# An attention and gated-MLP kernel: query blocks aligned to key tiles, and longer DMA transposes

## The chip, the cores and the metric

The kernel runs on one core of a Trainium2 chip. The metric is the device time of one execution in microseconds (us). A core has a matrix engine (TensorE, PE in the profile, with its weight loads shown as PEld), a vector engine (DVE), a scalar engine (ACT), GpSimd (POOL) and SyncE (SP), which here only issues transfers. Each engine works through its own queue in order and waits on semaphores. 16 DMA engines move data; transfers issued by SP, ACT and POOL share them. A profiled execution on the chip gives the rows quoted below.

## The reference

Eight batches with eight heads, 576 tokens each, head size 64. The keys and values are 16 beacon tokens, which every query sees, followed by the batch's own 576, which are causal. The attention output, with heads side by side, is the input of a gated MLP over all 4608 tokens.

```python
k_all = concat([beacon_k, k], axis=2)            # 16 + 576 keys
v_all = concat([beacon_v, v], axis=2)
scores = (q @ k_all.T) / sqrt(64)                # causal over the 576, beacons always seen
a = softmax(where(causal, -1e9, scores))
x = (a @ v_all)                                  # -> [4608, 512], 8 heads x 64 wide
out = (gelu(x @ w_gate) * (x @ w_val)) @ w_out   # 512 -> 1536 -> 512, output float32
```

Inputs are float32; inside, the kernel works in bfloat16 with float32 accumulation.

## The kernel before

**Attention.** Heads go in pairs, so that one pair's two heads of 64 stand in the two halves of the 128 partitions. A batch has four pairs (`m`). Queries and keys must stand with the head dimension on the partitions; that is `qkT`, one buffer for the batch at work. Scores are computed with keys on the partitions: for each of five key tiles (128, 128, 128, 128 and 80 rows, the first 16 of tile 0 being the beacons) against the queries that may see it. Because of the 16 beacons, the query blocks that start at a key tile's diagonal begin at 0, 112, 240, 368 and 496 (`S_LO`). A pair's scores come in four chunks (`CHUNKS`), each with one exponential on ACT; GpSimd then zeroes the masked triangle of each diagonal block (in batch 0 a matmul with `neg` does it). `attend` multiplies the exponentials with the values, with a column of ones that gives the denominator; DVE divides (`normalize`) and leaves `y_sb`, with query rows on the partitions and two heads side by side.

**Turning the result.** The MLP needs `xT_sb`, the model dimension on the partitions. In batches 1 to 7 the first three pairs are turned by DMA transposes on SP's queue (`turn_dma`, L368, two for each pair: 112 queries, then four blocks of 128). The fourth is turned by PE (`turn`, L180) and copied by DVE (`put`, L386). In batch 0 all four go through PE.

**Turning queries and keys.** Batches 0 and 1 are turned by PE (`tr_part`, tile `t_ps`). From batch 2 on, `transpose_dma` (L238) issues ten DMA transposes on SP's queue, five blocks of queries and five of keys, from buffers that GpSimd's transfers (L108, cast to bfloat16) filled one batch earlier.

**The MLP.** Nine chunks of 512 tokens (`ci`). `gate_val` makes one of 12 tiles of the hidden dimension: four matmuls for the gate, four for the value, GELU on ACT, product on DVE. `out_mms` makes the output; the matmuls of chunk b-1 are dealt out in portions, `o(n)`, between the attention steps of batch b, 48 in all for each batch.

**Order.** Every instruction's place is written out by hand and kept (`keep`). The loop over `b` has, in this order: ACT's table load, score chunks with portions of `out_mms`, `av_head` and `av` for the pairs, `turn_dma` for each, the fourth pair, the table load for GELU, then the first two gate tiles with the contraction steps `kk` in the order 0, 3, 1, 2, so that the pair whose DMA is last comes last. Then come the other ten tiles. After the first two tiles GpSimd's `hold` (L378) reads the columns of pair 2 in `xT_sb`: as POOL's queue is in order, the loads behind it (values of b+1, queries and keys of b+2) start only when that transpose has landed. The transposes of batch b+1 are issued in the same place. Stores of the output tiles go out where `store` stands, twice per batch on ACT's queue and twice on SP's. A DMA waits for the one eight places earlier on its kind of queue.

**The start.** The float32 queries and keys of batch 0's first pair come by SP's and ACT's queues into `raw` and are cast by ACT and DVE; all others come by GpSimd's transfers, already cast. 56 matmuls on zeros (`warm`) run on PE meanwhile, and eight filler transposes between the first key and query transposes.

Of the kernel before, what the change touches and what calls it, by code (L numbers as in the profile page):

```python
# [7 lines left out]
P = 128  # L8
B, H, S, NB, D = 8, 8, 576, 16, 64
SK = S + NB  # L10
# [11 lines left out]
S_LO = [0, 112, 240, 368, 496]  # L22
KROWS = [128, 128, 128, 128, 80]
DIAG = [112, 128, 128, 128, 80]
# [4 lines left out]
    [(0, 512, 64, 0), (2, 240, 336, 64), (4, 496, 80, 400)],  # L29
    [(1, 112, 464, 0)],  # L30
    [(3, 368, 208, 0)],
]
CHUNK_W = [512, 480, 464, 208]
CHUNK_OFF = [0, 512, 992, 1456]
EXP_W = 1664

EXP_OFF = [0, 992, 576, 1456, 912]
DV = D + 1

Q_N = [128, 128, 128, 128, 80]  # L40
# [11 lines left out]
def kernel(  # L52
# [17 lines left out]
    npool = ctx.enter_context(tc.tile_pool(name="npool", bufs=4))  # L70
    fpool = ctx.enter_context(tc.tile_pool(name="fpool", bufs=3))
# [14 lines left out]
    xT_sb = const.tile([P, NPAIR, N_TOK + P - Q_N[4]], BF16, name="xT_sb", tag="xT_sb")  # L86

    exp_ring = ring.tile([P, NPAIR, 2, EXP_W + P - Q_N[4]], BF16, name="expT", tag="expT")
# [13 lines left out]
    qkT = ring.tile([P, NPAIR, 2, 640], BF16, name="qkT", tag="qkT")  # L102
    nc.vector.memset(qkT[:, :, 1, SK:640], 0.0)

# [7 lines left out]
    def qk6_of(b):  # L112
        if b not in qk6:
            qk6[b] = (
                hpool.tile([P, 2, H, 6 * D], BF16, name="qk6", tag="hT_sb"),
                npool.tile([NB, H, D], BF16, name="kb", tag="kb"),
            )
        return qk6[b]
# [12 lines left out]
    def key_loads(src, beacon, dst, b):  # L131
        parts = [
            (dst[0:NB, 0, :, :], beacon[b].rearrange("h t d -> t h d")),
            (dst[NB:P, 0, :, :], src[b, :, 0:112, :].rearrange("h p d -> p h d")),
        ]
        for j in range(1, 5):
            n = KROWS[j]
            r0 = 112 + (j - 1) * P
            parts.append((dst[0:n, j, :, :], src[b, :, r0 : r0 + n, :].rearrange("h p d -> p h d")))
        return [lambda o=o, i=i: dma(o, i) for o, i in parts]  # L140

    def qk_loads(b):
        q_sb, k_sb = q_ring[b % NRING], k_ring[b % NRING]
        parts = []
        for j in range(5):
            n = P if j < 4 else 64
            parts.append(
                (q_sb[0:n, j, :, :], q[b, :, j * P : j * P + n, :].rearrange("h p d -> p h d"))
            )
        return [lambda o=o, i=i: dma(o, i) for o, i in parts] + key_loads(k, beacon_k, k_sb, b)  # L150
# [82 lines left out]
    def transpose_dma(b):  # L233
        q_sb, k_sb = q_ring[b % NRING], k_ring[b % NRING]
        for j in range(5):
            for w, src, n, c in ((0, q_sb, P if j < 4 else 64, NB), (1, k_sb, P if j < 4 else 80, 0)):
                keep(
                    nc.sync.dma_start_transpose(  # L238
                        out=qkT[:, :, w, c + j * P : c + j * P + n],
                        in_=src[0:n, j, :, :].rearrange("p h d -> p (h d)"),  # L240
                    )
                )

# [18 lines left out]
    def score_mms(b, m, c, s_ps):  # L262
        for t, s_lo, w, col in CHUNKS[c]:
            diag = b == 0 and s_lo == S_LO[t]
            for hi in range(2):
                r = slice(64 * hi, 64 * hi + 64)
                mm(
                    s_ps[:, hi, col : col + w],
                    qkT[r, m, 1, t * P : (t + 1) * P],
                    qkT[r, m, 0, NB + s_lo : NB + s_lo + w],  # L270
                    True,
                    not diag,
                    skip_group_check=True,
                )
            if diag:
                base, n = (NB if t == 0 else 0), DIAG[t]
                for k0, width in ((0, min(n, 64 - base)), (64, n)):
                    for hi in range(2):
                        r = slice(64 * hi, 64 * hi + 64)
                        c0 = 64 + 64 * hi - k0  # L280
                        mm(
                            s_ps[:, hi, col : col + width],
                            eye[r, c0 : c0 + P],
                            neg[r, c0 + base : c0 + base + width],
                            False,
                            k0 == 64,
                            skip_group_check=True,
                        )

    def masks(b, m, c):  # L290
        expT = exp_ring[:, m, :, :]
        for t, s_lo, _, _ in CHUNKS[c]:
            if s_lo != S_LO[t]:
                continue
            n = DIAG[t]
            d = expT[0 : KROWS[t], :, EXP_OFF[t] : EXP_OFF[t] + n]
            keep(
                nc.gpsimd.affine_select(  # L298
                    out=d,
                    in_=d,  # L300
                    pattern=[[0, 2], [1, n]],
                    compare_op=ALU.is_ge,
                    fill=0.0,
                    base=NB if t == 0 else 0,
                    channel_multiplier=-1,
                )
            )

    x_of = {}

    def attend(b, m, hi, x_ps):
        expT, v_sb = exp_ring[:, m, :, :], v_ring[b % NRING]
        for j in range(5):
            for t in range(j + 1):
                e0 = EXP_OFF[t] + S_LO[j] - S_LO[t]
                mm(
                    x_ps[:, j * DV : (j + 1) * DV],
                    expT[0 : KROWS[t], hi, e0 : e0 + P],
                    v_sb[0 : KROWS[t], t, 2 * m + hi, 0:DV],
                    t == 0,  # L320
                    t == j,
                    skip_group_check=True,
                )
# [3 lines left out]
    def normalize(b, m, x_ps, h0, h1):  # L327
        i = b * NPAIR + m
        if h0 == 0:
            y_of[i] = npool.tile([P, 5, 2, D], BF16, name="y_sb", tag="y_sb")  # L330
# [23 lines left out]

    def turn(b, m, pool=None, tag="t"):
        y_sb = y_of[b * NPAIR + m].rearrange("p j e d -> p j (e d)")
        y_ps = (pool or psum_t).tile([P, 1024], BF16, name="y_ps", tag=tag)
        y_of[b * NPAIR + m] = y_ps
        for j in range(5):
            n = Q_N[j] if j else S_LO[1]  # L360
            tr(y_ps[:, S_LO[j] : S_LO[j] + n], y_sb[0:n, j, :])

    def turn_dma(b, m):
        y_sb = y_of.pop(b * NPAIR + m)
        n0 = b * S
        for n, j0, j1, q0 in ((S_LO[1], 0, 1, 0), (P, 1, 5, S_LO[1])):
            keep(
                nc.sync.dma_start_transpose(  # L368
                    out=xT_sb[:, m, n0 + q0 : n0 + q0 + n * (j1 - j0)].rearrange("p (j n) -> p j n", n=n),
                    in_=y_sb[0:n, j0:j1, :, :].rearrange("p j e d -> p (j e d)"),  # L370
                )
            )

# [6 lines left out]
    def put(b, m, by_act=False):  # L380
        y_ps = y_of.pop(b * NPAIR + m)
        out_ap = xT_sb[:, m, b * S : (b + 1) * S]
        if by_act:
            act(out_ap, y_ps[:, 0:S], ACT.Copy)
        else:
            keep(nc.vector.tensor_copy(out_ap, y_ps[:, 0:S]))  # L386
# [87 lines left out]
    raw = [opool.tile([P, 4, D_MODEL], FP32, name="raw", tag="o_sb") for _ in range(2)]  # L474
    raw0 = [raw[w][0:96, 0:2, 0 : 6 * D] for w in range(2)]
    for w, engine in ((1, nc.sync), (0, nc.scalar)):
        keep(
            engine.dma_start(
                out=raw0[w], in_=(q, k)[w][0, 0:2, :, :].rearrange("h (p r) d -> p h (r d)", r=6)
            )  # L480
        )
    kb_sb, vb_sb = (raw[1][0:NB, g, :].rearrange("t (h d) -> t h d", h=H) for g in (2, 3))
    keep(nc.sync.dma_start(out=kb_sb, in_=beacon_k[0].rearrange("h t d -> t h d")))
    keep(nc.sync.dma_start(out=vb_sb, in_=beacon_v[0].rearrange("h t d -> t h d")))
    load_qk6(0, 2, 4, (1,))
# [39 lines left out]
    warm(56)  # L525
    act(qk6[0][0][0:96, 1, 0:2, :], raw0[1], ACT.Copy)
    keep(nc.vector.tensor_tensor_scan(neg, eye, idle, -1.0, ALU.add, ALU.add))
    keep(nc.vector.tensor_scalar_mul(neg, neg, -MASKED))
    keep(nc.vector.tensor_copy(qk6[0][1], kb_sb))
    keep(nc.vector.tensor_copy(qk6[0][0][0:96, 0, 0:2, :], raw0[0]))  # L530
    transpose_both(0, 0)
    keep(nc.vector.tensor_copy(v_ring[0][0:NB, 0, :, 0:D], vb_sb))
# [36 lines left out]
    for b in range(B):  # L569
# [6 lines left out]
        if b:  # L576
# [13 lines left out]
            store(nc.scalar)  # L590
# [14 lines left out]
            store(nc.scalar)  # L605
# [10 lines left out]
            o(7)  # L616
            store(nc.sync)
            turn(b, 3)
            put(b, 3)
            o(4)  # L620
            keep(nc.scalar.preload_act_table_set(SET_GELU))
            for kk in (0, 3, 1, 2):
                for fi in range(2):
                    gv_mms(b, fi, kk, last=kk == 2)
        for fi in range(F_TILES):
# [4 lines left out]
            if fi == 0:  # L630
                store(nc.sync)
                if b and b + 1 < B:
                    hold(b, 2)
# [3 lines left out]
                if 2 <= b + 1 < B:  # L637
                    transpose_dma(b + 1)
    for fi in range(F_TILES):
# [39 lines left out]
```

## Time and profile before

| | |
|---|---|
| time, median of 3 runs | 373.61 us (372.1 to 374.39) |
| the profiled execution's own time | 372.1 us |
| its span, first to last instruction | 370.4 us |
| PE busy | 360.1 us, 97% |
| ACT, POOL, DVE busy | 189.2, 159.7, 153.0 us |
| one batch, from first scores to first scores | 39.3 us (169.15 to 208.5) |
| PE in that batch: scores, attention, output, gate tiles | 4.03, 4.69, 11.27, 19.10 us |
| DMA queues, share of 16 engines: GpSimd's, SP's, ACT's | 68.0%, 25.5%, 4.1% |
| granted PE clock | half from 7.9 to 18.2 us, else full |

A busy row says how long at least one instruction of an engine was running. Shares of DMA engines count the time of every packet; they can add up to more than 1, since an engine has several packets under way. The chain of work that ended last goes back from the end: at each step to what released it. Its line names are those of the kernel printed above.

### The profile page before, as it was taken

What the parts mean: (1) busy time and instruction counts of PE and PEld (TensorE: products, weight loads), DVE (VectorE), ACT (ScalarE), POOL (GpSimd) and SP (SyncE); (2) the same over time, 40 slices, a digit from 0 to 9 for tenths busy, and PEclk for the clock granted to TensorE, in tenths of its full rate; (3) what the DMA queues carried; (4) which work ended last, traced back from release to release, by engine and by line L of the source; (5) the groups of instructions that cost most, each with busy time, mean ns of one, the idle gap of its engine ahead of it and who ended that gap; (6) DMA issues with size and microseconds to landing.
All of it is one profiled execution on the core that took longest, in us unless ns stands there. A gap on an engine that the chain in (4) does not pass through costs nothing.

```text
span 370.4 us, 7490 instructions
## 1 busy us (share of the span) xinstructions
PE 360.1 (97%) x3008; PEld 184.7 (50%) x3051; DVE 153.0 (41%) x278; ACT 189.2 (51%) x244; POOL 159.7 (43%) x286
## 2 busy tenths in 40 slices
PE   6999999999999999999999999999999999999996
PEld 5774545544554446444644455445544464444443
DVE  4453544433344435332534345333444353424332
ACT  3783379235933495339823792359334963331210
POOL 8834359482538443953457354835240430000000
PEclk9599999999999999999999999999999999999999
DMA  9999999999249984999289945992394041000103
GB/s 172 167 204 205 186 77 127 134 152 145 66 114 133 136 77 80 153 154 108 65 135 150 115 79 115 143 154 59 115 134 62 29 82 58 0 2 29 57 30 114
DMA packets 154900, 39.95 MB, mean 108 GB/s; under 512 B 141424, under 2 KB 150384, under 8 KB 154864
## 3 DMA queue, kind: packets, MB, share of 16 engines
q0 software_dynamic: 104432, 18.82, 68.0%
q1 hardware_dynamic: 48208, 16.67, 25.5%
q10 hardware_dynamic: 2224, 3.97, 4.1%
q8 instruction: 24, 0.39, 0.5%
q14 instruction: 12, 0.10, 0.1%
HBM read 38.27 MB, written 9.44 MB: 129 GB/s over the span
## 4 chain that ended last, share of the span: by engine, by line
PE 75%; DMA 15%; POOL 4%; issue 2%; DVE 2%; ACT 1%; SPq 0%; POOLq 0%; DVEq 0%
PE gv_ps L172 31%; PE o_ps L172 22%; PE x_ps L172 9%; PE s_ps L172 8%; DMA qkT<-k_sb 6%; DMA q_sb<-in_q_dram 5%; POOL v_sb L108 3%; PE t_ps L180 2%; DMA xT_sb<-y_sb 2%; DMA raw<-in_k_dram 1%; PE v_ps L172 1%; PE g_ps L172 1%; POOL q_sb L108 1%; PE y_ps L180 1%; DVE hT_sb L427 1%
## 5 line engine op out<-in xcount | busy, mean ns | idle before, releaser
L175 ACT ACTIVATE ge_sb<-gv_ps 128x512 bf16<-128x512 f32 x101 | 59.4, 597 | 144.5 <-PE gv_ps L172 142.5
L427 DVE TENSOR_TENSOR hT_sb<-gv_ps,ge_sb 128x512 bf16<-128x512 f32 x101 | 69.1, 691 | 115.4 <-ACT ge_sb L175 115.4
L172 PE MATMUL gv_ps<-xT_sb,wg_sb 128*128 128x512 bf16 x394 | 110.9, 379 | 0.5
L172 PE MATMUL gv_ps<-xT_sb,wv_sb 128*128 128x512 bf16 x401 | 110.9, 379 | 0.1
L175 ACT ACTIVATE expT<-s_ps 128x960 bf16<-128x960 f32 (+3 forms) x112 | 100.0, 963 | 10.4 <-PE s_ps L172 10.1
L172 PE MATMUL o_ps<-wo_sb,hT_sb 128*128 128x512 bf16 (+2 forms) x415 | 101.7, 373 | 1.4 <-issue 0.2
L298 POOL TENSOR_SCALAR_AFFINE_SELECT expT<-expT 128x256 bf16<-128x256 bf16 (+2 forms) x140 | 51.5, 384 | 73.4 <-ACT expT L175 72.6
L172 PEld LDWEIGHTS <-wv_sb 128*128 128x128 bf16 x432 | 42.3, 98 | 50.6
L172 PEld LDWEIGHTS <-wg_sb 128*128 128x128 bf16 x432 | 42.0, 98 | 50.0
L172 PEld LDWEIGHTS <-hT_sb 128*128 128x128 bf16 x444 | 38.8, 97 | 42.2 <-DVE y_sb L336 3.1
L172 PEld LDWEIGHTS <-expT 128*128 128x128 bf16 (+1 forms) x960 | 33.5, 97 | 10.7 <-DVE y_sb L336 4.0
L172 PE MATMUL s_ps<-qkT 64*128 64x512 bf16 (+5 forms) x384 | 35.6, 292 | 2.3 <-ACT qkT L175 0.7
L172 PE MATMUL x_ps<-v_sb,expT 128*128 128x65 bf16 (+1 forms) x960 | 37.1, 193 | 0.0
L108 POOL DMA_DIRECT2D v_sb<-in_v_dram x40 | 34.1, 870 | 6.8 <-DMA wv_sb<-in_moe_w_val_dram 1.7
L446 DVE COPY o_sb<-o_ps 128x512 f32<-128x512 f32 (+2 forms) x37 | 25.0, 676 | 27.2 <-PE o_ps L172 26.1
L108 POOL DMA_DIRECT2D k_sb<-in_k_dram x30 | 25.2, 842 | 17.2 <-DMA q_sb<-in_q_dram 10.9
L336 DVE TENSOR_TENSOR y_sb<-x_ps,r_sb 128x320 bf16<-128x320 f32 (+1 forms) x47 | 28.8, 612 | 1.6
L334 DVE RECIPROCAL r_sb<-x_ps 128x5 f32<-128x5 f32 (+1 forms) x47 | 9.6, 204 | 46.8 <-PE x_ps L172 46.8
L108 POOL DMA_DIRECT2D q_sb<-in_q_dram x30 | 25.3, 886 | 3.5 <-DMA wo_sb<-in_moe_w_out_dram 3.5
L172 PEld LDWEIGHTS <-qkT 64*128 64x128 bf16 x384 | 14.9, 96 | 18.6 <-issue 12.0
L378 POOL COPY hold_sb<-xT_sb 128x2 bf16<-128x2 bf16 x6 | 1.1, 186 | 29.5 <-DMA xT_sb<-y_sb 29.5
L180 PE MATMUL t_ps<-eye,qk 96*64 96x96 bf16 x192 | 8.0, 236 | 1.6 <-ACT qk L175 1.6
(51 smaller groups left out, 124.4 us busy)
## 6 DMA issues: line engine op xcount, KB each, us to landing
out_dram<-o_sb SPq DMA_DIRECT2D x21, 256.0 KB, 2.4
out_dram<-o_sb ACTq DMA_DIRECT2D x14, 256.0 KB, 3.1
v_sb<-in_v_dram POOLq DMA_DIRECT2D x24, 128.0 KB, 6.0
q_sb<-in_q_dram POOLq DMA_DIRECT2D x24, 128.0 KB, 8.6
k_sb<-in_k_dram POOLq DMA_DIRECT2D x18, 128.0 KB, 9.2
wo_sb<-in_moe_w_out_dram POOLq DMA_DIRECT2D x3, 512.0 KB, 14.7
wg_sb<-in_moe_w_gate_dram POOLq DMA_DIRECT2D x2, 512.0 KB, 11.3
wv_sb<-in_moe_w_val_dram POOLq DMA_DIRECT2D x2, 512.0 KB, 12.8
```

The lines of the kernel that those rows point to most:

```text
L108: keep(nc.gpsimd.dma_start(out=out_ap, in_=in_ap))
L172: keep(nc.tensor.matmul(out_ap, lhsT, rhs, start=start, stop=stop, **kw))
L175: keep(nc.scalar.activation(out_ap, in_ap, func, **kw))
L180: keep(nc.tensor.transpose(out_ap, in_ap, ident[0:n, 0:n]))
L298: nc.gpsimd.affine_select(out=d, in_=d, pattern=[[0, 2], [1, n]], compare_op=ALU.is_ge, fill=0.0, base=NB if t == 0 else 0, channel_multip ...
L334: keep(nc.vector.reciprocal(r, x[:, :, :, D:DV]))
L336: nc.vector.tensor_tensor(out=y_of[i][:, :, h0:h1, :].rearrange("p j b d -> p b j d"), in0=x[:, :, :, 0:D], in1=r.to_broadcast([P, h1 - h0 ...
L378: keep(nc.gpsimd.tensor_copy(hold_sb, x[:, 0 : S : S - 1]))
L427: nc.vector.tensor_tensor(out=h_of[ci][:, fi, :], in0=gv_of.pop((ci, fi))[1], in1=ge_sb, op=ALU.mult)
L446: keep(nc.vector.tensor_copy(o_sb[:, ti, c0:c1], o_ps))
```

## The change

- The query blocks start at multiples of 128 like the key tiles: 16 unused query places stand in front (`LO` in place of `S_LO`). In `xT_sb` the first 16 columns of a batch's window are then the last 16 of the batch before; a small DVE copy puts those rows into `y_sb` first. The second chunk is 496 wide in place of 480.
- `transpose_dma` turns all queries of a batch with one DMA of 20 blocks and all keys with another, into a layout ordered by tile (`qkT_by_tile`). For batches 2 to 7 a query range that crosses column 512 is cut in two score matmuls.
- `turn_dma` turns a pair by one DMA of five blocks, and is used for the fourth pair too; `turn` and `put` stay for batch 0. The first two gate tiles take `kk` in the order 0, 1, 2, 3, behind eleven output matmuls, and `hold` reads pair 3.
- All four stores of a batch go out together on SP's queue, behind the two transposes.
- The first pair's queries and keys come by GpSimd's transfers ahead of the others; `raw` and its casts go. There are 66 warm-up matmuls, and seven more memsets on DVE for the padding.

```diff
     def transpose_dma(b):
-        for j in range(5):
-            for w, src, n, c in ((0, q_sb, P if j < 4 else 64, NB), (1, k_sb, P if j < 4 else 80, 0)):
-                keep(
-                    nc.sync.dma_start_transpose(
-                        out=qkT[:, :, w, c + j * P : c + j * P + n],
-                        in_=src[0:n, j, :, :].rearrange("p h d -> p (h d)"),
-                    )
+        for w, ring_w in ((0, q_ring), (1, k_ring)):
+            keep(
+                nc.sync.dma_start_transpose(
+                    out=qkT_by_tile[:, w].rearrange("p j m c -> p (j m) c"),
+                    in_=ring_w[b % NRING].rearrange("p j h d -> p (j h d)"),
                 )
+            )
...
     def score_mms(b, m, c, s_ps):
...
+            if b < 2:
+                pieces = [(lo, lo + w)]
+            else:
+                pieces = [(c0, c1) for c0, c1 in ((lo, min(lo + w, 512)), (max(lo, 512), lo + w)) if c0 < c1]
...
     def turn_dma(b, m):
-        y_sb = y_of.pop(b * NPAIR + m)
-        n0 = b * S
-        for n, j0, j1, q0 in ((S_LO[1], 0, 1, 0), (P, 1, 5, S_LO[1])):
-            keep(
-                nc.sync.dma_start_transpose(
-                    out=xT_sb[:, m, n0 + q0 : n0 + q0 + n * (j1 - j0)].rearrange("p (j n) -> p j n", n=n),
-                    in_=y_sb[0:n, j0:j1, :, :].rearrange("p j e d -> p (j e d)"),
-                )
-            )
+        y_sb, y_before = y_of[b * NPAIR + m], y_of.pop((b - 1) * NPAIR + m)
+        keep(nc.vector.tensor_copy(y_sb[0:NB, 0, :, :], y_before[KROWS[4] - NB : KROWS[4], 4, :, :]))
+        c0 = b * S - NB
+        keep(
+            nc.sync.dma_start_transpose(
+                out=xT_sb[:, m, c0 : c0 + 5 * P].rearrange("p (j n) -> p j n", n=P),
+                in_=y_sb.rearrange("p j e d -> p (j e d)"),
+            )
+        )
...
-    for w, engine in ((1, nc.sync), (0, nc.scalar)):
-        keep(
-            engine.dma_start(
-                out=raw0[w], in_=(q, k)[w][0, 0:2, :, :].rearrange("h (p r) d -> p h (r d)", r=6)
-            )
-        )
...
+    load_qk6(0, 0, 2)
     load_qk6(0, 2, 4, (1,))
...
-    warm(56)
-    act(qk6[0][0][0:96, 1, 0:2, :], raw0[1], ACT.Copy)
+    warm(66)
...
             scores(b, (1, 2))
-            store(nc.scalar)
...
             av(b, 3)
-            o(7)
-            store(nc.sync)
-            turn(b, 3)
-            put(b, 3)
-            o(4)
+            turn_dma(b, 3)
+            o(11)
             keep(nc.scalar.preload_act_table_set(SET_GELU))
-            for kk in (0, 3, 1, 2):
+            for kk in range(K_CHUNKS):
                 for fi in range(2):
-                    gv_mms(b, fi, kk, last=kk == 2)
+                    gv_mms(b, fi, kk, last=kk == 3)
...
             if fi == 0:
-                store(nc.sync)
                 if b and b + 1 < B:
-                    hold(b, 2)
+                    hold(b, 3)
                     load_v(b + 1)
                 if b and b + 2 < B:
                     load_qk(b + 2)
                 if 2 <= b + 1 < B:
                     transpose_dma(b + 1)
+                store(nc.sync)
```

## The prediction

> **What bounds the kernel now.** I read the busy table first, then the stage table of one batch, then the chain that ended last, then the queues. In the busy table TensorE (PE) stands alone, and the clock row shows one cold slice near the start:
>
> ```profile
> PE 360.1 (97%) x3008; PEld 184.7 (50%) x3051; DVE 153.0 (41%) x278; ACT 189.2 (51%) x244; POOL 159.7 (43%) x286
> PEclk9599999999999999999999999999999999999999
> ```
>
> Only 10.3 us of the 370.4 us span are without a running matmul: 3.5 before 8.1 us, 3.3 in the tail after 326.5. So little can be won by better overlap after the start; what counts is work put on PE or taken off it, and any new wait of PE. The stage table of the fifth batch (b = 4; columns: stretch and length in us, then busy time and count on PE, weight load, DVE, ACT, POOL, then clock, DMA share, GB/s) has its attention stage, the stretch of its fourth pair's turn, and its gate stage:
>
> ```profile
> 169.15:184.40 15.25, 15.13 (x200) 8.64 (x203) 5.87 (x13) 14.03 (x16) 7.38 (x20) 1.00 0.52 72
> 184.40:186.80 2.40, 2.35 (x15) 1.23 (x15) 1.50 (x3) 0.00 (x0) 0.00 (x0) 1.00 0.36 67
> 186.80:208.50 21.70, 21.52 (x99) 9.70 (x99) 8.87 (x13) 8.04 (x13) 13.82 (x18) 1.00 1.69 147
> ```
>
> PE is full in all three. ACT is near its limit in attention alone; the DMA share is over 1 in the gate stage, where loads and transposes share the 16 engines. The chain shows what those transposes are worth (start, length):
>
> ```profile
> 184.66 0.83 DVE y_sb L336
> ...
> 186.07 2.49 DMA xT_sb<-y_sb
> ...
> 201.04 8.29 DMA qkT<-k_sb
> 209.59 2.05 PE o_ps L172 x9
> ```
>
> The last of ten query/key transposes lands at 209.33, just when the scores, begun at 208.5, want the last key tile. In the table of waits PE's weight load lost only 1.3 us to them in the whole run (4 times). It is a close race that PE wins or loses by tenths.
>
> **The change, part by part.** Sums are against the profiled execution: 372.1 us, of which 370.4 are span. The median of the three times is 373.61, 1.5 more.
>
> *Fourth pair turned by DMA.* Seven batches lose five PE transposes and a DVE copy. From PE's timeline:
>
> ```profile
> 185.72 0.42 PE L180 MATMUL y_ps<-eye,y_sb 112*128 112x112 bf16 x5
> 185.98 1.03 PE L172 MATMUL o_ps<-wo_sb,hT_sb 128*128 128x512 bf16 x3
> ```
>
> By the starts the five cost 0.26 us of PE, all on the path: 7 x 0.27 with the gap before them = **-1.9 us**. What is late next is the DMA of this pair, since the last contraction step (kk = 3) of the first two gate tiles now reads it. Attention ends on PE at 184.39. Then: division done 185.48 (DVE row above), new copy of 16 rows 0.15 (the 128x16 copies at L221 take 0.14 to 0.16), SyncE issue at about 185.7, and 2.5 us to landing as in the chain plus 0.15 for the fifth block: 188.35. PE first has 11 output matmuls and 12 gate matmuls at 0.216 each (13 in 2.81 us in the chain): 184.39 + 4.97 = 189.36. That hides it with 1.0 us to spare. Three of the 21 second-piece issues took 1.8 to 2.2 us instead of 1.26; even that fits. If cover were gone, each further us would cost 7.
>
> *GpSimd's hold* (L378) now waits for pair 3: 188.35 in place of 188.56, so the loads behind it in POOL's queue do not move.
>
> *Query and key transposes: two issues of 20 blocks for ten of 4.* Issuing is SyncE's time: 1.12 us for one block, 1.26 for four, ten times about 1.4 now. By that slope, 20 blocks take about 2.0. What the engines do is seen in two windows of the DMA view (queue, packets, MB, share): 2.5 us with transposes alone, then 8 us with loads beside them.
>
> ```profile
> q1 hardware_dynamic: 2219, 0.53, 124.9%
> ```
> ```profile
> q0 software_dynamic: 4975, 0.62, 121.3%
> q1 hardware_dynamic: 2589, 0.61, 61.0%
> ```
>
> That is 888 packets per us alone and 324 beside loads (276 in 190 to 204, 215 in 192 to 200). A batch has 4672 such packets now and 5120 padded. First packets come when the issue ends: 187.0 + 2 = 189.0; the loads' first packets are at 190.3. So some 1150 go alone, and 3970 at 276 need 14.4 us: landed at about 204.7, against 208.5 when the scores start. The scores must now wait for the whole of both DMAs, but the two stores no longer stand before them on SyncE. **-0.2 us** for the small waits that go. At 215 per us it is 208.8, the edge; this is rival C.
>
> *Stores.* Four per batch behind the transposes on SyncE's ring. Two leave ACT's queue (0.34 to 0.40 us each in a stage where ACT is 92% busy): that more than pays for exponentials that are 32 elements wider on four of 14 instructions (0.963 us per 960 elements, so 0.13 us per batch). 128 packets of 2 KB add about 1.4 us of DMA time for the pair of stores that came from ACT, after the transposes. The loads then end at about 214 instead of 212; GpSimd's last issue, at 165.0 in the batch of the 147.6 us stage, has 5 us before the next mask. Cost 0; with the cover gone, masks, and so attention, would slip.
>
> *Score matmuls in pieces.* From b = 2 a head pair has 18 instead of 12, since a query range crossing 512 is cut: 12 more instruction pairs (two row halves side by side) per batch, and 16 more columns per head pair in all batches. Columns: 16 x 4 x 8 x 0.42 ns = 0.2 us. A piece costs what a short matmul costs beyond its columns. By the start times at 214.35, a 64-wide pair is followed after 39 ns, 336 after 143, 80 after 35; at 0.42 ns per column 27, 141 and 34 are the columns. So 1 to 12 ns each; the highest reading is a run of twelve score matmuls, 0.88 us for 1408 columns, (0.88 - 0.594)/6 = 48 ns. Bounds 0 and 12 x 6 x 48 = +3.4 us. I take 5 ns, nearest to the 80-wide row that the pieces are: +0.4. Together **+0.6 us**. The strided query operand isn't in this trace; its price lies inside the same upper bound.
>
> For this the Trainium skill speaks against the change: "TensorE: Matmul & The Clock Gate", section Back-to-back issue gap, gives some 81 ns sustained per weight load and matmul at 128 columns, which by my estimate would be 12 x 6 x 81 = +5.8 us and turn the whole change into +3. The trace has 120 attention matmuls 65 wide, each with its own weights, in 4.69 us, 39 ns each, so I don't take it.
>
> *The start.* The first head pair came as float32 by SyncE's and ACT's queues and was cast; now it comes cast by GpSimd's, in front of the others.
>
> ```profile
> 1.38 0.77 POOL L108 DMA_DIRECT2D qk<-in_k_dram  x1 [0.85 <-POOLq L663]
> ...
> 5.05 0.84 ACT L175 ACTIVATE qk<-raw 96x768 bf16<-96x768 f32 x1 [2.50 <-DMA raw<-in_k_dram]
> ...
> 5.95 0.45 PE L180 MATMUL t_ps<-eye,qk 96*64 96x96 bf16 x12 [1.65 <-ACT qk L175]
> ...
> 8.07 0.61 PE L172 MATMUL s_ps<-qkT 64*128 64x512 bf16 x2 [0.75 <-ACT qkT L175]
> ```
>
> GpSimd's first load (issued 1.38) landed at 6.63 and its second at 6.95, but behind 576 KB of float32 that are gone now. Its first packet came 2.6 us after issue; later loads' come after 1.2 to 1.6. Worst case, the same landings: key transposes at 6.65, scores at 8.8, +0.75. Best case: first packet at 2.7, landed 4.4, query 5.1, key transposes at 4.7 when the 66 warm-ups (54 ns each) end, 0.5 us, filler 0.4, query transposes to 6.1, ACT's copy 0.65 (ACT row of the trace), scores at 6.95: -1.1. DVE must keep up: seven more memsets (0.15 to 0.3 by the 0.22 us rows), beacon casts 0.42 + 0.89, mask 0.92, key copy 0.74, done about 6.8, so no later. I take -0.8, near the best case because the bytes in front are gone: **-0.8 us**. GpSimd's other loads go out 1.3 us later; first weights are wanted at 25.1 and landed at 16.2, first values at 19.8 and landed at 14.9.
>
> The Trainium skill, "DMA: Bandwidth & Descriptors", section Latency and other measured facts, has the first byte at 1 us by GpSimd against 0.6 by the others, against this step; by that gap alone, an estimate, the start would lose 0.4 us. The trace has 1.0 against 2.6 here, and the cast saved is 0.84.
>
> Sum: -1.9 - 0.2 + 0.6 - 0.8 = **-2.3 us**: 369.8 beside the profiled 372.1, and 371.3 beside the median. A difference under 1% (3.7 us) is about what a measurement of this kernel can't tell from none.
>
> **The rivals.**
> *A, the sum:* 371.3, chance 0.48.
> *B, the clock stays up.* The trace has the granted clock at half from 7.93 to 18.17 us, after a stretch in which PE idled 1.65 + 0.75 us. The shorter gaps might keep it up. ACT is busy 7.3 of these 10 us, so at most 2.7 go: 368.6. Against it: 64-row score matmuls at 90% busy didn't raise it for 7 us. Chance 0.15.
> *C, slower: the two long transposes land after the scores want them,* because one deep queue beside deep loads gets less than its share, or the 20-block form runs slower. Place: the first scores of b = 2 to 6 (the last transposes have no query loads beside them). Point: 208.5 - 190.3 for 3970 packets, under 218 per us, a hair over the lowest row, which SyncE's issuing still held back in part. Price: at 170 per us 5 us late, five times; at 190, 2.7 us x 5 = +13.5 on the sum, 384.8. Chance 0.13; I add 0.04 for the fourth pair landing over 1.5 us late (7 x 0.5, 375).
> *D, no gain:* the pieces cost 30 ns each (+1.8 more) and the start gains nothing: 373.9. Also the case that the change does its work and PE's saved 1.9 us is paid back. Chance 0.20.
>
> **How the numbers follow.** Predicted: A, 371.3. Lowest bound: 373.6 - 1.9 - 0.2 + 0.2 - 1.1 - 2.7 = 367.9; highest without C: 373.6 - 1.9 + 0.2 + 3.4 + 0.75 = 376.1. I give 367.8 to 376.2, which leaves out C. Faster by over 1% (under 369.9): B and a tenth of the chance from A's lower half, 0.25. Slower (over 377.3): C and a little, 0.16. Within: 0.59.
>
> **What would show it.** PE transposes of y_ps only in the first batch (20 instead of 55 instructions); 144 more score matmuls, their busy time per batch near 4 us as now; two 20-block issues of about 2 us per batch and the landing before the scores; PE without a gap ahead of kk = 3 (else the fourth pair is late); first scores near 7.2 us. Wrong would be: a PE gap at each batch's first scores (C), score spacing of 40 ns a piece (D), another length of the half-clock stretch (B).

## The result, and the profile after

The changed kernel takes **367.91 us** (367.77 to 367.99, four runs) where the kernel before takes 373.47 beside it (372.1 to 374.39): a ratio of **0.9854** [0.9823, 0.9885], 1.46% faster. The forecast was 371.3 in a range of 367.8 to 376.2. The time lies just inside the range's lower end, where the prediction had put rival B, the clock that stays up (368.6). Its likeliest case, A, was 3.4 us too slow, and a time within 1% of the kernel before, to which it gave 0.59, did not come.

The profiled execution took 367.98 us, with a span of 366.2 against 370.4. These are lines of its page: busy time, the granted clock in 40 slices, SyncE's DMA queue (packets, MB, share of 16 engines), the shares of the chain that ended last, and the score matmuls (busy, mean ns | idle before).

```profile
PE 355.5 (97%) x3127; PEld 183.6 (50%) x3170; DVE 154.8 (42%) x305; ACT 188.8 (52%) x243; POOL 161.7 (44%) x288
...
PEclk9999999999999999999999999999999999999999
...
q1 hardware_dynamic: 55536, 21.96, 29.7%
...
PE 94%; DVE 2%; DMA 1%; issue 1%; POOL 1%; POOLq 0%
...
L173 PE MATMUL s_ps<-qkT 64*128 64x80 bf16 (+5 forms) x528 | 34.1, 250 | 2.4 <-DVE qkT L222 1.3
```

The clock row has no 5 left in its second slice. The chain that ended last is PE's own for 94%; before it was 75%, and DMA held 15%, most of it transposes of keys (6%) and loads of queries (5%). 144 more score matmuls are busy for less time (34.1 us, 35.6 before), but that is the first batch, whose clock is now full (7.6 us before, 5.8 after); in a later batch both kernels show 4.04 to 4.09 us.

**Where the 4.2 us of span went.** Two places hold all of it. By the starts on PE, the first score matmul comes at 6.97 us (8.07 before) and the second batch's scores at 47.45 (50.09): 2.64 us are gained in the start, of them 1.10 ahead of the first scores and 1.54 behind. From then on each batch is shorter by 0.16 to 0.34 us: 39.16 us in every one of batches 2 to 6, against 39.32 to 39.50. The 1.54 us behind the first scores are not work taken away; the windows view shows what they are. Its columns are the window, its length, and the busy time (and instructions) of PE, PEld, DVE, ACT and POOL, then PE's granted clock, the DMA share and GB/s. First before, then after:

```profile
0.00:8.00 8.00, 4.54 (x89) 4.26 (x90) 3.96 (x13) 2.75 (x3) 6.74 (x14) 1.00 0.89 168
8.00:18.20 10.20, 9.96 (x153) 6.83 (x154) 4.23 (x9) 7.30 (x9) 9.11 (x13) 0.50 1.77 169
```

```profile
0.00:8.00 8.00, 5.95 (x123) 5.40 (x123) 5.04 (x19) 2.45 (x3) 6.75 (x15) 1.00 0.72 96
8.00:18.20 10.20, 8.03 (x203) 5.94 (x198) 5.38 (x13) 9.52 (x12) 9.42 (x13) 1.00 1.72 168
```

In the same 10.2 us PE does 203 instructions in place of 153, with less busy time, since its clock is full and not half. ACT becomes the busy engine there (9.52 of 10.20). By the records of the clock, before was full from 4.52 to 7.93 and half until 18.17; after it is full from 4.35 to the end. (Ahead of its first record a trace doesn't tell the clock, so "else full" in the table of the kernel before holds from 4.52 us only.)

The fourth pair came in time, as the prediction had it. These are pieces of the chain of work of the changed kernel in order of time (start, length), and the instruction on GpSimd that reads the last transposed pair:

```profile
181.09 2.38 PE o_ps L173 x11
183.47 0.65 PE gv_ps L173 x3
184.11 0.05 issue
184.16 10.74 PE gv_ps L173 x49
```

```profile
185.18 0.19 POOL L382 COPY hold_sb<-xT_sb 128x2 bf16<-128x2 bf16 x1 [5.17 <-DMA xT_sb<-y_sb]
```

The transpose landed at 185.06. The fourth contraction step comes after twelve gate matmuls of 0.2155 us, at 183.47 + 2.59 = 186.06. PE runs through with 0.05 us of issue and no wait, and the margin, counted as the prediction did along the chain, is its 1.0 us. By the matmuls' own starts it is 0.8 (0.7 in two batches).

SyncE's queue in the same batch, and the two long transposes over all batches (min/median/max ns):

```profile
178.28 5.41 SPq L372 DMA_TRANSPOSE xT_sb<-y_sb  x3
183.97 3.09 SPq L237 DMA_TRANSPOSE qkT<-q_sb  x1
187.74 5.00 SPq L237 DMA_TRANSPOSE qkT<-k_sb  x1
192.81 2.07 SPq L458 DMA_DIRECT2D out_dram<-o_sb  x4
```

```profile
L237 SPq DMA_TRANSPOSE qkT<-q_sb x6: 3073/3088/3097, 66.6 to 262.4; - x6
L237 SPq DMA_TRANSPOSE qkT<-k_sb x6: 4522/5038/5122, 70.0 to 265.7; - x6
```

The long issues take 3.1 and 5.0 us, not the estimated 2.0 each. Yet the queries landed at 191.26 and the keys at 199.13, 5.9 us ahead of the scores at 205.05; over all batches the spare time is 5.6 to 7.0 us. Before, the last transpose landed 0.37 to 0.81 us behind the start of the scores in five batches of six.

### The profile page after: what moved, and what is told of

It is laid out like the page before. It is cut to its first block, busy times and chain, and to the rows that moved or that the text cites. A ratio compares the mean times of both kernels' runs of the same rounds, so it can differ in the third digit from the quotient of the medians.

```text
span 366.2 us, 7625 instructions
## 1 busy us (share of the span) xinstructions
PE 355.5 (97%) x3127; PEld 183.6 (50%) x3170; DVE 154.8 (42%) x305; ACT 188.8 (52%) x243; POOL 161.7 (44%) x288
## 4 chain that ended last, share of the span: by engine, by line
PE 94%; DVE 2%; DMA 1%; issue 1%; POOL 1%; POOLq 0%
PE gv_ps L173 47%; PE o_ps L173 25%; PE x_ps L173 9%; PE s_ps L173 8%; PE v_ps L173 2%; PE g_ps L173 2%; DMA qk<-in_q_dram 1%; PE t_ps L181 1%; DVE qkT L218 1%; POOL qk L116 0%; PE y_ps L181 0%; DVE qkT L200 0%; DVE qkT L204 0%; POOL eye L485 0%; DVE o_sb L450 0%
## 5 line engine op out<-in xcount | busy, mean ns | idle before, releaser
L173 PE MATMUL gv_ps<-xT_sb,wv_sb 128*128 128x512 bf16 x388 | 107.9, 379 | 0.4
L176 ACT ACTIVATE expT<-s_ps 128x992 bf16<-128x992 f32 (+3 forms) x112 | 100.5, 973 | 8.7 <-PE s_ps L173 8.5
L173 PE MATMUL o_ps<-wo_sb,hT_sb 128*128 128x512 bf16 (+2 forms) x420 | 100.6, 373 | 2.1 <-issue 1.1
L303 POOL TENSOR_SCALAR_AFFINE_SELECT expT<-expT 128x256 bf16<-128x256 bf16 (+1 forms) x140 | 52.6, 392 | 53.6 <-ACT expT L176 50.5
L173 PEld LDWEIGHTS <-hT_sb 128*128 128x128 bf16 x444 | 39.3, 98 | 43.1 <-DVE y_sb L339 3.1
L173 PE MATMUL s_ps<-qkT 64*128 64x80 bf16 (+5 forms) x528 | 34.1, 250 | 2.4 <-DVE qkT L222 1.3
L173 PEld LDWEIGHTS <-qkT 64*128 64x128 bf16 x528 | 17.1, 95 | 18.8 <-issue 12.4
```

Source lines behind the costliest of these rows:

```text
L173: keep(nc.tensor.matmul(out_ap, lhsT, rhs, start=start, stop=stop, **kw))
L176: keep(nc.scalar.activation(out_ap, in_ap, func, **kw))
L303: nc.gpsimd.affine_select(out=d, in_=d, pattern=[[0, 2], [1, n]], compare_op=ALU.is_ge, fill=0.0, base=0, channel_multiplier=-1,)
```

## The experiments

All times are medians; each ratio is to runs of the kernel before on the same chip in the same set, whose medians were 374.7 (`e1` to `e4`), 373.95 (`e5` to `e8`) and 373.48 (`e11`, `e12`).

| | time, us | ratio | a batch (2 to 6), us |
|---|---|---|---|
| `e1`: before, new start alone | 369.06 | 0.9886 [0.9855, 0.9917] | 39.32 to 39.84 |
| `e2`: after, old start | 372.73 | 0.9957 [0.9933, 0.9981] | 39.16 |
| `e3`: after, 56 warm-ups | 368.23 | 0.9856 [0.9834, 0.9878] | 39.16 |
| `e4`: before, 88 warm-ups | 369.91 | 0.9893 [0.9866, 0.9920] | 39.32 to 40.23 |
| `e5`: after, fourth pair by PE | 369.35 | 0.9880 [0.9845, 0.9916] | 39.42 |
| `e6`: after, pieces of 128 | 368.04 | 0.9848 [0.9812, 0.9884] | 39.18 |
| `e7`: after, ten transposes | 367.60 | 0.9833 [0.9797, 0.9868] | 39.16 (one 39.34) |
| `e8`: after, stores first | 367.64 | 0.9831 [0.9789, 0.9873] | 39.16 |
| `e12`: after, ten transposes and stores first | 383.14 | 1.0252 [1.0228, 1.0276] | 40.9 to 44.2 |
| `e11`: after, 30 warm-ups | 370.11 | 0.9901 [0.9881, 0.9921] | 39.16 |

### The start: alone, and undone

`e1` puts the new start into the kernel before; `e2` gives the changed kernel the old one.

```diff
-    raw0 = [raw[w][0:96, 0:2, 0 : 6 * D] for w in range(2)]
...
+    load_qk6(0, 0, 2)
     load_qk6(0, 2, 4, (1,))
...
-    warm(56)
-    act(qk6[0][0][0:96, 1, 0:2, :], raw0[1], ACT.Copy)
+    warm(66)
```

> The kernel before with the new start alone: first pair by GpSimd's transfers, 66 warm-ups, the casts in their new order; nothing else is changed. Theory S (the start is worth 2.6 us by the markers of the two traces: first gate matmul at 24.2 in place of 26.9, of which 1.1 is the earlier first score and 1.5 the half-clock stage that is gone): span about 367.8, time 2.6 under the profiled 372.1 of before and about 4 under its median; clock full from 4.4 on, first scores at 7.0. Rival T (the start gain is paid for by the seven memsets' absence or by batch 0's ACT chain, and the rest of the change carries the difference): first scores early, but first gate matmul within 0.5 us of 26.9.

> The changed kernel with the old start: float32 first pair by SyncE's and ACT's queues, cast by ACT and DVE, 56 warm-ups. Theory S: what is left is the batches' share, 7 x 0.27 less the pieces: batches from first scores to first scores 39.15 in place of 39.4, time 1.5 to 2.0 under before; a half-clock stage of about 10 us after 7.9 is back. Rival T: time within 1 us of the changed kernel, 367.9.

The start alone is worth 1.14%, the rest of the change 0.43%; together 1.57%, against 1.46% for the whole. So the two parts add up, and the start is the larger one. In `e1` the clock is full from 4.63 us and the first scores are at 6.86; in `e2` it is not up before 17.35 and the scores are at 8.99. The batches tell the parts apart in the same way: 39.16 in `e2`, 39.3 to 39.8 in `e1`.

### The clock: more warm-ups before, fewer after

`e3` takes the ten added warm-ups away again; `e4` leaves the kernel before as it is, but adds 32 warm-ups; `e11` stops the changed kernel's warm-ups at 2.9 us.

```diff
# e3, in the changed kernel
-    warm(66)
+    warm(56)
# e4, in the kernel before
-    warm(56)
+    warm(88)
# e11, in the changed kernel
-    warm(66)
+    warm(30)
```

> The changed kernel with 56 warm-up matmuls in place of 66, which end at 4.1 in place of 4.7 us; key transposes still at about 4.85. If the ten warm-ups keep the clock up (theory W), the half-clock stage returns and the time is 1.5 to 2.7 us longer, about 370. If the shorter wait for the first pair does it (theory L), the gap of 0.7 us changes nothing and the time stays at 367.9.

> The kernel before with 88 warm-up matmuls in place of 56: PE runs on to about 5.9 us, where the first transposes start, so the 1.65 us gap is closed and nothing else is changed; first scores stay at 8.07. If the gap lets the clock fall, the half-clock stage goes and the time drops by 1.5 to 2.7 us, to about 371. If the later gap before the scores or the transposes themselves let it fall, the time stays at 373.5.

> The kernel after with 30 warm-up matmuls in place of 66: TensorE then idles from about 2.8 us until the first transposes at 4.6 to 4.9 us, and nothing else changes; the loads, the casts and the landings are those of the kernel after. Theory K (of the start's gain the clock is the larger part): the granted clock isn't up at 4.4 us but rises only at 13 to 18 us, the first scores start near 7.0 to 7.7 us, and the first gate tile near 26 to 27 us instead of 24.22; the time is 2 to 5 us longer than that of the kernel after, 370 to 373 us. Rival L (the gain is the shorter way of the first queries and keys into TensorE, whatever the clock): 367.7 to 368.7 us, the gate tile at 24 to 25 us. Batches 39.16 us apart under both.

56 warm-ups do as well as 66 (368.23; in the trace the clock is full from 4.02 us), so the shorter gap behind them is enough and the ten are not needed in these runs. `e4` moves no load and no cast, and its first scores come later (8.63); still its first gate tile starts at 22.96, against 25.09 in before's trace, and it is 1.07% faster. Its warm-ups didn't close the gap as expected: they end at 5.15 us, and PE then idles 1.27 us, yet the clock stays full from 4.00. Those 32 matmuls alone thus bring nearly what the whole new start brings in `e1` (1.14%). That is 4.0 us by the ratio, more than the clock's share in `e11` below; before's own runs in that set lie between 372.9 and 376.88, and no run shows where the rest of it comes from. The clean test is `e11`, the same loads without the clock. This is PE's timeline of `e11`, then its windows:

```profile
1.13 1.78 PE L173 MATMUL w_ps<-idle 128*128 128x64 bf16 x30 [1.13 <-DVE idle L80]
4.73 0.69 PE L181 MATMUL t_ps<-eye,qk 96*64 96x96 bf16 x12 [1.82 <-DMA qk<-in_k_dram]
```

```profile
8.00:18.20 10.20, 10.04 (x163) 6.95 (x161) 4.25 (x8) 7.42 (x9) 8.97 (x12) 1.00 1.78 175
```

The clock column reads 1.00 since no earlier record says otherwise; the first record is a rise to full at 17.80. That the clock was half shows in the work: twelve transposes take 0.69 us where the changed kernel takes 0.45, and PE does 163 instructions in 10.2 us, not 203. The first gate tile starts at 24.84 us, against 22.45 in the changed kernel, and the time is 370.11: **2.2 us in the medians, 1.8 by the ratios and 2.4 in the traces are the clock's**, and theory K holds. (The gate tile's 24.22 in the expectation was counted along the chain of work, and by that count it is 26.61 in `e11`; 22.45 and 24.84 are first starts.) The rest of the gain, 3.4 us, is there without the clock.

### The kernel before, executed twice more

Both are the kernel before, unchanged, for one profile each (373.42 and 373.8 us).

> The kernel before, unchanged, executed once more with a profile, to see how its granted clock and its batches differ from one execution to the next. Theory W (the clock rises at the end of a window of about 3.4 us in which TensorE was busy enough, and where the windows lie differs from one execution to the next): the first stretch of full clock begins and ends elsewhere than in the execution profiled before (4.52 to 7.93 us, half until 18.17), and may be missing until 17 to 18 us; the first gate tile then starts between 24.5 and 29 us instead of 26.86, and the distances from one batch's scores to the next lie between 39.3 and 40.3 us, since its short transposes land about when the scores want them. Rival F (the clock's record is a fixed answer to this instruction order): full clock begins within 0.1 us of 4.52 and ends within 0.1 us of 7.93 again, the gate tile at 26.8 to 26.9, and the batches at 39.3 to 39.5.

> The kernel before, unchanged, a second execution beside the first, for the same two theories. W: the stretches of full clock differ from those of the first by more than 0.3 us or by a whole window of 3.4 us, and the distances between batches scatter between 39.3 and 40.3 us. F: the same records as in the first to 0.1 us.

The record is not fixed: F falls. In these two, full clock begins only at 16.82 and 19.05 us; the stretch from 4.52 to 7.93 that the prediction had read is missing. And the batches are longer than the prediction's 39.3: 39.32 to 40.03 from batch 2 on. Both traces show the same reason, here as the chain of waits of the first of the two:

```profile
155.37 8.58 DMA q_sb<-in_q_dram
163.95 7.10 DMA qkT<-k_sb
171.05 0.05 issue
171.09 0.21 PE s_ps L172 x2
```

The scores of this batch began at 169.70, and the last key transpose landed at 171.05. Set beside the length of the batch, the landing gives a simple rule. Late by 0.37, 0.49 or 0.62 us costs nothing (39.32); 0.78, 0.93, 1.23 and 1.35 cost 0.14, 0.29, 0.59 and 0.71: everything beyond 0.64 us is paid one for one. Over the batches that is 0.38 us in the execution profiled before, 1.59 and 1.21 in these two.

With the last matmul's end as the measure, the kernels then stand in a row. Each step is one part of the change, from one trace each:

| | last matmul ends, us | step |
|---|---|---|
| before, the two executions above | 368.65, 369.04 | |
| after with the old start (`e2`; clock at 17.35) | 366.87 | -2.0: all of the change but the start; late transposes gone, fourth pair by DMA |
| after with 30 warm-ups (`e11`; clock at 17.80) | 365.54 | -1.3: shorter way in (0.6 at the first gate tile); the second batch is 0.7 shorter, for no reason that the runs show |
| after | 363.12 | -2.4: the clock |

### The fourth pair, and the pieces

`e5` gives the fourth pair back to PE; `e6` cuts the scores into pieces of at most 128 columns, 24 more pairs of matmuls in each batch from the third.

```diff
# e5
-            turn_dma(b, 3)
-            o(11)
+            o(7)
+            turn(b, 3)
+            put(b, 3)
+            o(4)
...
# e6
-                pieces = [(c0, c1) for c0, c1 in ((lo, min(lo + w, 512)), (max(lo, 512), lo + w)) if c0 < c1]
+                pieces = [(c0, min(c0 + P, lo + w)) for c0 in range(lo, lo + w, P)]
```

> The changed kernel with the fourth pair of batches 1 to 7 turned by PE and copied by DVE again, the old order of the contraction steps and the hold on pair 2. By the prediction's step this costs 7 x 0.27 = 1.9 us: batches of 39.43 in place of 39.16 us, time about 369.8. Rival: the five transposes were already hidden in PE's waits, or the fourth pair's DMA costs as much as it saves: within 0.4 us of the changed kernel.

> The changed kernel with every score range of batches 2 to 7 cut at each multiple of 128: 15 instruction pairs for a head pair in place of 9, 144 pairs more in the run. At 1 to 5 ns a piece (the prediction's reading of the start times) the time rises by 0.1 to 0.7 us; at the upper bound of 48 ns it rises by 6.9 us to about 375; at 35 ns, the shortest spacing seen in front of another matmul, it would rise by 5.

`e5` adds 0.26 us to each batch (39.42), which is the line that the prediction had priced at 0.27. (The median is 1.4 us longer, less than the 1.8 of seven batches; in the traces its first batch is 0.9 us shorter than the changed kernel's.) From its PE timeline, the five transposes are back and take 182.46 to 182.72:

```profile
182.46 0.42 PE L181 MATMUL y_ps<-eye,y_sb 128*128 128x128 bf16 x5
182.72 1.03 PE L173 MATMUL o_ps<-wo_sb,hT_sb 128*128 128x512 bf16 x4
```

`e6` adds 0.02 us to each batch, 0.9 ns for each of 24 more pairs. In the changed kernel itself, scores, attention and output matmuls take 18.44 us of PE in a batch, against 18.34 before (by their starts, in undisturbed batches): 0.10 us for twelve pieces and 64 more columns. Less 0.03 us for the columns at 0.42 ns each, that is at most 6 ns a piece. 39.32 - 0.26 + 0.10 is the measured 39.16.

### The two long transposes, and the stores behind them

`e7` turns queries and keys by ten transposes again, in the new layout; `e8` sends the four stores ahead of the two long transposes; `e12` does both.

```diff
# e7
+            for j in range(5):
                 nc.sync.dma_start_transpose(
-                    out=qkT_by_tile[:, w].rearrange("p j m c -> p (j m) c"),
+                    out=qkT_by_tile[:, w, j],
...
# e8
             if fi == 0:
+                store(nc.sync)
...
                     transpose_dma(b + 1)
-                store(nc.sync)
```

> The changed kernel with ten transposes of four blocks for queries and keys, into the new layout, all queries first, in place of the two of 20 blocks. Theory R (the old form loses a close race in some batches and executions): SyncE issues for 14 us, the last transpose lands at or after the first scores, batches scatter between 39.2 and 40.2 us and the time rises by 0.5 to 2 us. Rival: what PE sees is set by bytes, not by the number of transfers: batches stay at 39.16, time within 0.3 us of the changed kernel.

> The changed kernel with the four stores issued on SyncE's queue ahead of the two transposes of queries and keys, not behind them. The transposes landed at 199.1 in the fifth batch, 5.9 us before the scores; four issues (2.1 us) and 1 MB ahead of them (5 us at the rate of the stores in the trace) take about all of that. If the place of the stores matters only through this race, the landing comes at 204 to 206 and the time rises by 0 to 2 us; if the stores in front also hold back the loads or the fourth pair, by more.

> The kernel after with both orders on SyncE undone at once: ten transposes of one block row each in place of two long ones, in the new layout, query's first, and the four result stores ahead of them. Each alone left the batches 39.16 us apart, with the last transpose landing from 0.85 us after to 2.2 us ahead of the score matmuls. Theory S (the long DMAs and the stores last are spare cover that neither edit alone used up): together they miss the scores, the last transposes land 0.5 to 2 us after the first scores' start in most batches, the distances between batches scatter between 39.2 and 40.2 us, and the time is 0.5 to 3 us above 367.6, so 368.1 to 370.6 us. Rival N (there is nothing to win in the order of the queue, since the first score matmuls read only the first blocks): batches at 39.16 us in spite of later landings, 367.4 to 368.0 us.

Each edit alone costs no time: 367.60 and 367.64, by their intervals no different from the changed kernel. Taken alone, the long DMAs bring nothing, and the theory that they do falls. The two edits only use up spare time: the last landing is 0.9 us behind to 1.1 us ahead of the scores in `e7` (6.5 in the last batch, which has no query and key loads beside it), and 0.2 to 1.7 us ahead in `e8` (4.7 in the last). Both together cost **15.2 us**: theory S in kind, but far above the 0.5 to 3 that it expected. SyncE's queue of `e12` in one batch:

```profile
183.09 9.82 SPq L373 DMA_TRANSPOSE xT_sb<-y_sb  x4
192.97 2.04 SPq L459 DMA_DIRECT2D out_dram<-o_sb  x4
195.11 7.99 SPq L238 DMA_TRANSPOSE qkT<-q_sb  x5
203.20 7.42 SPq L238 DMA_TRANSPOSE qkT<-k_sb  x5
```

The ten issues take 15.4 us and end at 210.6; the landing is 6 us later, 2.4 us behind the scores at 214.21. In the other batches it is 3.0 to 4.1 us late, and beyond 0.64 us this is paid one for one, as in before. In two batches more is paid, as the windows of `e12` show:

```profile
130.09:133.50 3.41, 1.24 (x8) 0.60 (x9) 0.00 (x0) 1.36 (x2) 0.48 (x2) 1.00 2.14 153
133.50:136.91 3.41, 3.41 (x20) 1.20 (x19) 0.69 (x1) 1.02 (x3) 0.70 (x3) 0.50 0.08 5
171.05:174.46 3.41, 2.02 (x19) 0.77 (x16) 0.77 (x2) 3.18 (x4) 0.40 (x1) 1.00 1.81 149
174.46:177.87 3.41, 2.12 (x11) 0.90 (x11) 0.04 (x1) 1.18 (x2) 1.08 (x3) 1.00 1.58 104
```

Where PE was busy for 1.24 of 3.41 us, the clock is half in the next window of 3.41; that costs 1.6 us more, and the two batches in which it happens are 44.1 and 44.2 us long. In a third batch a gap of 2.69 us falls across the border of two windows, which leaves 2.02 and 2.12 us busy; the clock stays, and the batch is 41.9 us.

No version is clearly faster than the changed kernel: 367.60, 367.64 and 367.91 can't be told apart.

## Why the prediction was right or wrong

**Fourth pair: right.** -1.9 us was 7 x 0.27; `e5` gives 0.26 a batch. Its cover was priced at 1.0 us and is 1.0.

**Score pieces: right in sum, with the price of a piece too high.** Priced at +0.6; the 0.10 us a batch makes 0.7 over seven batches. `e6` puts a further piece at 0.9 ns, not 5; which part of the 0.10 is then the strided operand, the wider columns or something else, no run tells. The rule of the Trainium skill that the prediction had weighed ("TensorE: Matmul & The Clock Gate", Back-to-back issue gap) would have given +5.8 by estimate, and nothing of the kind is seen.

**Query and key transposes: the right result by wrong sizes.** The issues take 3.1 and 5.0 us, not 2.0 each. The first packets came at 185.14, 1.2 us after the first issue began, and not at its end. The queries' 2560 packets went in 3.4 us, nearly all ahead of the loads' first at 188.49 (762 per us, not 888; in before the loads' first came at 190.78, not 190.3), and the keys' 2560 in 5.6 us beside the loads (458 per us, not 276). The keys landed 5.9 us ahead of the scores, where the forecast had 3.8 (204.7 against 208.5), so rival C had 2.1 us more to make up than the prediction saw. The gain of "-0.2 us for the small waits" was 0.38 by the trace that the prediction used, but 1.2 to 1.6 in two other executions of the same kernel. This term was mis-sized, because a landing within 1 us of its use was read from a single execution.

**Stores: cost 0, right, with less cover than it gave.** GpSimd's last load issue ended at 204.7 with the next mask at 206.57: 1.9 us of the 5 are left. (The pair of stores from ACT is 256 packets of 2 KB by the trace; the prediction counted 128, those of one.) What the stores' place is worth was not seen at all. The step put them "after the transposes" at no cost; it did not ask what they would cost ahead of them. `e12` answers: in the changed kernel, either the long transposes or the stores behind them must be there.

**The start's way in: right.** -0.8 was forecast from a best case with first scores at 6.95; they came at 6.97. At half clock they come at 7.76 in `e11`, 1.1 and 1.2 us earlier than in the two executions of before; at the first gate tile (24.84) 0.4 and 1.1 us of that are left, and against `e2` 0.6.

**The clock: the step that failed.** The size was right: "at most 2.7", and 1.8 to 2.4 by `e11`. The step that failed is the argument by which the sum left the clock out, with a chance of 0.15 for it. "64-row score matmuls at 90% busy didn't raise it for 7 us" speaks of raising a clock that is down; the question was whether one that is up would fall. It fell after windows in which PE was busy for 40% or less, and stayed after 51% and more (last section). These are the windows view's lines for the first window at full clock, before and after:

```profile
4.52:7.93 3.41, 1.38 (x33) 1.25 (x34) 2.17 (x5) 1.40 (x2) 3.41 (x4) 1.00 1.30 195
```

```profile
4.35:7.76 3.41, 2.49 (x59) 1.97 (x58) 1.95 (x5) 0.93 (x2) 3.41 (x6) 1.00 1.08 141
```

In before PE is busy for 1.38 of 3.41 us, 40%, with the idle 1.65 and 0.75 us at the window's two ends; after, for 73%. After the change, by the prediction's own best case, the first of the two gaps was nearly gone (warm-ups to 4.7, key transposes from 4.7). With the clock's 2.4 us and the 1.0 to 1.4 that the late transposes cost beyond the forecast's 0.2, A's 371.3 becomes 367.5 to 367.9. That the time still lies in the range is partly luck: the bound of 367.9 takes the pieces at 0.2 us (0.7 measured) and the clock at 2.7 (1.8 to 2.4), and it leaves out the 1.0 to 1.4 us of the late transposes.

## What to carry to other kernels

Ask of a short idle time on PE early in a kernel not only how long it is, but what the clock does after it, and price both; some 35 more warm-up matmuls were worth 2 us in the changed kernel and 4 in the one before. Where a transfer lands within 1 us of its use, one profile doesn't say what it costs: two more executions of the same kernel showed three and four times as much. And an edit that measures nothing when undone alone may still hold the kernel up together with another: undo them together before calling them free.

## What the runs showed that was not expected

**The clock moves in windows of 3.413 us that don't start with the kernel.** Every stretch of full clock between two records is a whole number of them (361.81 = 106, 354.99 = 104, 129.71 = 38), and the first rise lay at 3.79, 4.00, 4.02, 4.35, 4.52, 4.54, 4.63, 4.97, 5.87, 16.82, 17.35, 17.80 or 19.05 us (one trace has no record). This agrees with the Trainium skill, "TensorE: Matmul & The Clock Gate", Part 1, which has a free-running window of 3413 ns. The runs add shares, by the profile's busy time of PE. Warm-up matmuls that filled 78% of a first window raised the clock (`e12`), 75% didn't (`e2`). At half clock, windows filled to 94 to 96% by transposes and 64-row scores didn't raise it, and 100% did, in five executions; why those need more is open. A clock that was up stayed up after windows filled to 51, 59, 61 and 62%, and fell after 26 and 36% (`e12`) and 40% (before). The same page's table Why this matters for your kernels warns of idle gaps over some 3 us; here 2.0 to 2.5 us of idle time inside one window were enough, and 2.69 us across two were not. That the seven runs of before beside the last experiments scatter by 2.3 us, and those of the changed kernel by 0.2, would fit windows that fall differently on the first gaps, and late transposes as well. The granted clocks of before's 27 runs beside the experiments go with the first: the 13 with 0.985 or 0.986, as in the execution profiled first, have a mean of 373.6 us, the 14 with 0.999 or 1.0, as in the two later ones, 374.6. But in `e2` the same two groups are 0.2 us apart, so this stays open.

**Transposes on PE count towards staying up.** In the changed kernel's window from 4.35 to 7.76 us, matmuls other than transposes fill 30% and transposes 43% (in `e3`'s first window at full clock 21 and 40%), and the clock stayed; at 36% without transposes it fell in `e12`. Part 4 of the same page has transposes not counting as busy in the same way; for staying up, these windows speak against it.
